# Handing out the mirror transposes of an attention kernel at two fixed keys of a block pair

## The chip, the cores and the metric

The kernel runs on one core of one Trainium2 chip. The metric is the device time of one execution in microseconds. A core has five engines that work side by side, each through its own queue in order: TensorE (PE, with its weight loads shown as PEld), VectorE (DVE), ScalarE (ACT), GpSimd (POOL) and SyncE (SP), which here only issues DMA transfers. Engines wait for each other and for transfers by semaphores.

## The reference

Eight batches of squared-relu attention without a softmax, gated by `u`, and then a mixture of experts over all 22528 tokens, with one dense expert and the best of eight gated ones:

```python
# u, v: (8, 2816, 256); z: (8, 2816, 64); scale = 1 / 2816
scores = scale * np.matmul(z, z.transpose(0, 2, 1))
attn = np.maximum(scores, 0.0) ** 2
x = (u * np.matmul(attn, v)).reshape(22528, 256)
y_dense = np.maximum(x @ w1_dense, 0.0) @ w2_dense
e = argmax(x @ w_gate);  gate = its softmax probability
out = y_dense + gate * (np.maximum(x @ w1[e], 0.0) @ w2[e])
```

The scores are those of `z` with itself, so `attn` is symmetric: the block of queries i and keys k is the transpose of the block of queries k and keys i.

## The kernel before, in words

**Tiles and groups.** A batch has 2816 positions, 22 blocks of 128 (`nK`). Queries are taken in groups of 2, 4, 4, 4, 4 and 4 blocks (`groups`), keys in blocks of 128. A group's squared scores stand in a buffer `A[n]` of 22 key blocks by up to 512 queries in bf16; three such buffers turn (`aA`, `bufs=3`), so group n+3 writes where group n was.

**Scores.** `scores` multiplies two key blocks with the queries of a group into a pair of PSUM banks (L383); `relu` offers two steps: the relu with the scale (ScalarE L398 or VectorE L400) into one of five `r` buffers, and the square (ScalarE L411, VectorE L413, or GpSimd in the first two groups) into `A[n]`. Four pairs of banks serve scores and outputs together.

**Mirror transposes.** Of a group n with n-2 in the same batch, the key blocks that belong to the queries of group n-2 aren't computed: they are the transposes of blocks that stand in `A[n-2]`. `far_steps(a)` makes the steps for that, four for each of the groups 0 to 3 of a batch; each is one DMA transpose, issued on SP (L446), that reads one key block of `A[a]` and writes columns of `A[a+2]`. There are 128 in the program. The last step of a group sets `key_at` for the mirrored blocks, the time at which the planner takes them as there.

**Outputs.** `av(n, i, ...)` multiplies a pair of query blocks (i, i+1) of group n with v: two halves (p = 0, 1) of 22 keys (x), four matmuls each (L552) with 64 rows. In the first half of a group's first pair the keys are taken in the order of their `key_at`. Between the keys it fills in scores of this group or the next two (`fill`). Behind a pair comes the gate (`gate_x`, VectorE L579), which multiplies the output by `u` into `pays` and then issues the transpose of the result on SP (L581, `xT`), which the router's logits (TensorE L607) need later.

**The order.** All engine queues but GpSimd's are in the order in which the Python code calls the instructions; a planner with a clock of its own (`now`, costs of the steps, `free`) decides while it runs which of the offered steps comes next and on which engine. At the start of `av`, `turning.extend(far_steps(n))` puts the group's four steps at the end of a list, and after a key the first of the list is taken, if the planner holds that its squares are done and that group a+1 is open.

**SP's queue.** It holds, in order, for every pair: the load of `u` for two pairs later (L146, three `ut` buffers, so it waits for the gate that frees one), the `xT` of an earlier pair (L581), the mirror transposes (L446), and twice a batch a transpose of z for the next batch (L116, `zT`), which waits for a copy on VectorE (L113).

**Then the mixture of experts.** Tokens are scattered by expert during the attention (GpSimd L697); after it, from about 562 us, the expert tiles are computed (L897 to L935). The change touches nothing there.

Of the kernel before, what the change touches and what calls it, by code (L numbers as in the profile page):

```python
# [19 lines left out]
def kernel(  # L20
# [63 lines left out]
    def banks(x, name, shape=(P, 2, 4 * P), dt=F32):  # L84

        return ps.tile(list(shape), dt, name=name, tag=f"b{x}")
# [46 lines left out]
    now = [0.0]  # L133
# [7 lines left out]
    def load_u(g, gate=False):  # L141
        ut = aw.tile([P, 2, D], F32, name="ut", bufs=3)
        if gate:
            nc.vector.memset(ut[:, 0, 0:1], 0.0)
        b, i = divmod(g, nK)
        nc.sync.dma_start(out=ut[:], in_=uf[:, b, i:i + 2, :])  # L146
        ut_of[g] = ut[:]
# [134 lines left out]
    def offer(ready, rank, ways, then=None):  # L282
        count[0] += 1
        todo.append((rank, count[0], ready, ways, then))
# [44 lines left out]
    def until(cond):  # L329

        while cond() is None:
            pick = best()
            assert pick is not None
            now[0] = max(now[0], pick[0][0])
            give(pick)
        now[0] = max(now[0], cond())
        run(now[0])

    def pe(t):
        now[0] += t  # L340
        run(now[0])


    left, far, key_at = {}, {}, {}
# [7 lines left out]
    def open_group(n):  # L352
        if n not in A:
            A[n] = aA.tile([P, nK, 4 * P], BF, name="A", tag="A")
# [6 lines left out]
    def take_pair():  # L361
        return pairs.pop(0)[1]

    def give_pair(t, x):
        pairs.append((t, x))
        pairs.sort()
# [64 lines left out]
    def can_turn(n, m):  # L431
        _, i0, w = groups[n]
        ts = [key_at.get((m, k)) for k in range(i0, i0 + w)]
        return None if None in ts else max(ts)

    def far_steps(a):

        n = a + 2
        if n >= len(groups) or far[n] != [a]:
            return []  # L440
        (b, i0, w), (_, j0, wj) = groups[n], groups[a]

        def step(i):
            assert n - 1 in A
            open_group(n)
            nc.sync.dma_start_transpose(out=A[n][:, j0:j0 + wj, i * P:(i + 1) * P],  # L446
                                        in_=A[a][:, i0 + i, :wj * P])
            if i == w - 1:
                for j in range(wj):
                    key_at[n, j0 + j] = now[0] + 10.0  # L450

        return [(a, lambda i=i: step(i)) for i in range(w)]

# [2 lines left out]
    def fill(n, force=False):  # L456

        if jobs and jobs[0][0] <= now[0] and room(1):
            jobs.pop(0)[1]()
            return True  # L460
        m = ahead(n)
        busy = sum(1 for op in todo if op[0] in (1, 4))
        if m is not None and room(1) and busy <= (4 if n < 2 else 2):
            scores(m, left[m].pop(0))
            return True
        return False
# [7 lines left out]
    def v_at(n, k):  # L474

        return 3.3 + 2.6 * (4 * k // nK) if n == 0 else 0.0

    def need(n, k):

        while max(key_at.get((n, k), 9e9), v_at(n, k)) > now[0]:  # L480
            if fill(n):
                continue
            pick = best()
            ts = [t for t, _ in pairs if t > now[0]]
            ts += [max(key_at[n, k], v_at(n, k))] if (n, k) in key_at else []
            assert pick is not None or ts
            if pick is not None and (not ts or pick[0][0] <= min(ts)):
                now[0] = max(now[0], pick[0][0])
                give(pick)
            else:  # L490
                now[0] = min(ts)
        run(now[0])

    turning = []
# [8 lines left out]
    def swap_rows(n):  # L503

        keep[0] = 0
        if ahead(n) is None:
            until(lambda: pairs[0][0] if pairs else None)
            x = take_pair()
            touch(x)
            touch(x)  # L510
            give_pair(now[0] + 0.1, x)
            return
        until(lambda: pairs[1][0] if len(pairs) > 1 else None)
        x = take_pair()
        touch(x)
        m = ahead(n)
        scores(m, left[m].pop(0))
        m = ahead(n)
        if m is None:
            touch(x)  # L520
            give_pair(now[0] + 0.1, x)
        else:
            scores(m, left[m].pop(0), x)

    def av(n, i, between):
        b, i0, w = groups[n]
        if i == i0:
            turning.extend(far_steps(n))
        keep[0] = 0
        if n == 0 and i == i0:  # L530

            fill(n)
            need(n, 0)
        until(lambda: pairs[0][0] if pairs else None)
        ox = take_pair()
        o = banks(ox, "o")
        for p in range(2):
            rest = list(range(nK))
            for x in range(nK):
                k = rest[0]  # L540
                if i == i0 and p == 0:

                    k = min(rest, key=lambda k: (max(key_at.get((n, k), 9e9), v_at(n, k)), k))
                    need(n, k)
                rest.remove(k)
                if n == 0 and i == i0 and p == 0 and x in (12, 14, 16):
                    load_u(2 * (x - 12) // 2, gate=True)
                for h in range(2):
                    r = slice(h * dq, (h + 1) * dq)
                    j = p ^ h  # L550
                    c = (i + j - i0) * P
                    nc.tensor.matmul(out=o[:, j, 0:D], lhsT=A[n][r, k, c:c + P],  # L552
                                     rhs=v_of[b][r, k, :], start=(p == 0 and x == 0),
                                     stop=(p == 1 and x == nK - 1))
                pe(0.1092)
                keep[0] = 2 - p if x >= nK - 12 else 0
                if x % 2 == 1 and x < nK - 1:
                    fill(n)
                if x % 7 == 3 and turning:
                    t = can_turn(turning[0][0] + 2, turning[0][0])  # L560
                    if t is not None and t <= now[0] and turning[0][0] + 1 in A:
                        turning.pop(0)[1]()
            if p == 0:
                swap_rows(n)
                between()

        def done(t):
            give_pair(t + 0.1, ox)

        g = b * nK + i  # L570
        offer(now[0] + 0.2, 0, {"dve": (0.63, lambda eng: gate_x(g, o))}, done)
        keep[0] = 0


    def gate_x(g, o):
        g0 = g % (2 * G)
        x = pays[:, g0:g0 + 2, 0:D]
        assert g + 1 < 2 * G or (g - 2 * G in placed and g + 1 - 2 * G in placed)
        nc.vector.tensor_mul(x, o[:, :, 0:D], ut_of.pop(g))  # L579
        xT = aw.tile([P, 5, P], BF, name="xT", bufs=8)  # L580
        nc.sync.dma_start_transpose(  # L581
            out=xT[:], in_=pays[:, g0:g0 + 2, :].rearrange("p n r -> p (n r)")[:, 0:5 * P])
        for j in range(2):
            xT_of[g + j] = xT[:, 3 * j:3 * j + 2, :]
# [512 lines left out]
    for n, (b, i0, w) in enumerate(groups):  # L1097
        for i in range(i0, i0 + w, 2):
            g = b * nK + i
            if 0 < g < nB - 4:  # L1100
                load_u(g + 4)
            av(n, i, lambda: tick(g))
            tick(g + 1)
# [7 lines left out]
    for s in range(NT - MAYBE + 2):  # L1111
# [4 lines left out]
        if s % 3 == 1 and waiting:  # L1116
# [5 lines left out]
    n = nc.values_load(used[0:1, 0:1], min_val=0, max_val=NH,  # L1122
                       skip_runtime_bounds_check_because="made by the table")
# [34 lines left out]
```

## Time and profile before

| | us |
|---|---|
| median of 3 runs | 886.56 |
| all three runs | 884.21, 886.56, 899.62 |
| the profiled execution | 887.47 |
| its span on the engines | 885.8 |

The profile is of one execution. A group row gives the line, the engine, the operation, what it writes and reads, the count, the busy time and the mean duration. A timeline row begins with start and duration in us; equal instructions that follow each other are merged into one row with their count, and square brackets hold the engine's idle time before the row and what ended it. A row of waits reads: who waited for whom, us in total, times, longest. SPq is SP's queue; its rows are issues, and a transfer lands later than its issue ends. The clock that TensorE was granted is 0.994 of full speed.

### The profile page before, as it was taken

How to read it: one execution, taken by the hardware profiler on the slowest of the kernel's cores; microseconds unless marked ns; L12 is line 12 of the kernel's file. 1: busy time of each engine (PE TensorE's matmuls, PEld its weight loads, DVE VectorE, ACT ScalarE, POOL GpSimd, SP SyncE). 2: the span in 40 equal slices, each digit the busy share in tenths (PEclk: the TensorE clock that was granted, in tenths of full speed). 3: DMA queues.
4: the chain of work that ended last, by engine and by line, in shares of the span. 5: the costliest groups of instructions: out<-in, count | busy, mean ns of one | idle time of the engine just before them, and what ended most of it. 6: DMA issues, size and time to landing. Idle time of an engine off the chain costs nothing.

```text
span 885.8 us, 30592 instructions
## 1 busy us (share of the span) xinstructions
PE 864.5 (98%) x12257; PEld 759.7 (86%) x12257; DVE 701.2 (79%) x1320; ACT 738.6 (83%) x913; POOL 485.2 (55%) x532
## 2 busy tenths in 40 slices
PE   8999999999998999999999999999999999999996
PEld 5788888898886888888888888888888888889996
DVE  7999999998996999999998997656665445546664
ACT  7999998998996998998998997477777777777774
POOL 8203343434533534434434544488888888887665
PEclk9999999999999999999999999999999999999998
DMA  6795997998898899899899896555565555544333
GB/s 148 148 174 117 146 185 145 172 174 170 153 165 168 154 181 190 127 197 198 131 196 172 151 159 112 103 133 128 129 132 122 117 120 121 123 113 110 97 100 82
DMA packets 257871, 127.64 MB, mean 144 GB/s; under 512 B 225470, under 2 KB 232894, under 8 KB 257728
## 3 DMA queue, kind: packets, MB, share of 16 engines
q1 hardware_dynamic: 230112, 70.24, 47.6%
q0 software_dynamic: 27616, 55.44, 29.2%
q8 instruction: 96, 1.57, 0.8%
q14 instruction: 47, 0.39, 0.2%
HBM read 61.54 MB, written 37.16 MB: 111 GB/s over the span
## 4 chain that ended last, share of the span: by engine, by line
PE 73%; DVE 7%; issue 6%; POOL 6%; DMA 4%; ACT 3%; SPq 0%; POOLq 0%; DVEq 0%; ACTq 0%
PE o L552 37%; PE h_ps L909 14%; PE yy L917 13%; PE s L383 8%; POOL out_dram L935 5%; DMA xT<-pays 3%; DVE r L400 2%; DVE A L413 2%; ACT A L411 1%; POOL A L413 1%; PE lg L607 1%; ACT r L398 1%; DVE pays L579 1%; DMA out_dram<-ring,ix 1%; DVE zn L113 1%
## 5 line engine op out<-in xcount | busy, mean ns | idle before, releaser
L552 PE MATMUL o<-vb,A 64*128 64x256 bf16 x7744 | 493.7, 270 | 2.6 <-POOL A L413 1.8
L552 PEld LDWEIGHTS <-A 64*128 64x128 bf16 x7744 | 408.1, 94 | 53.9 <-POOL A L413 3.0
L697 POOL DMA_INDIRECT xs<-pays,pi x176 | 196.9, 1119 | 271.1 <-DVE pi L695 207.1
L398 ACT ACTIVATE r<-s 128x1024 f32<-128x1024 f32 x274 | 270.0, 1011 | 26.1 <-PE s L383 22.1
L411 ACT ACTIVATE A<-r 128x1024 bf16<-128x1024 f32 (+1 forms) x257 | 261.3, 1042 | 5.3 <-DMA A<-A 2.7
L912 ACT ACTIVATE ring<-h_ps 128x1024 bf16<-128x1024 f32 x180 | 183.9, 1023 | 89.2 <-PE h_ps L909 87.3
L413 DVE TENSOR_TENSOR A<-r 128x1024 bf16<-128x1024 f32 x167 | 201.8, 1221 | 5.8 <-DMA A<-A 4.0
L400 DVE TENSOR_SCALAR r<-s 128x1024 f32<-128x1024 f32 (+1 forms) x158 | 190.5, 1214 | 4.3 <-POOL A L413 1.8
L933 DVE SCALAR_TENSOR_TENSOR ring<-yy,me,ring 128x256 f32<-128x256 f32 x180 | 86.8, 482 | 123.0 <-ACT ring L932 86.3
L935 POOL DMA_INDIRECT out_dram<-ring,me x140 | 146.4, 1046 | 39.8 <-issue 23.5
L383 PE MATMUL s<-zT 64*128 64x512 bf16 (+1 forms) x944 | 157.9, 359 | 1.6 <-ACT zT L192 0.6
L917 PEld LDWEIGHTS <-ring 128*128 128x128 bf16 x1440 | 140.0, 98 | 16.2 <-issue 0.3
L917 PE MATMUL yy<-w2d,ring 128*128 128x256 bf16 x720 | 108.0, 273 | 0.1
L917 PE MATMUL yy<-ring 128*128 128x256 bf16 x720 | 108.0, 273 | 0.0
L909 PE MATMUL h_ps<-ring,w1d 128*128 128x256 bf16 x720 | 93.3, 273 | 0.8 <-DVE pays L579 0.8
L909 PE MATMUL h_ps<-ring 128*128 128x256 bf16 (+1 forms) x880 | 93.7, 253 | 0.0
L897 DVE COPY ring<-wall 128x2048 bf16 x110 | 80.7, 748 | 8.6 <-DVE ring L933 4.2
L909 PEld LDWEIGHTS <-ring 128*128 128x128 bf16 x880 | 74.3, 98 | 6.8
L909 PEld LDWEIGHTS <-w1d 128*128 128x128 bf16 x720 | 70.1, 98 | 9.0 <-issue 1.0
L579 DVE TENSOR_TENSOR pays<-o,ut 128x512 bf16<-128x512 f32 x88 | 60.3, 685 | 17.6 <-PE o L552 17.1
L383 PEld LDWEIGHTS <-zT 64*128 64x128 bf16 x944 | 58.0, 94 | 16.0 <-issue 3.4
L932 ACT COPY ring<-yy 128x256 f32<-128x256 f32 x180 | 66.1, 367 | 1.8 <-PE yy L917 1.8
(120 smaller groups left out, 358.0 us busy)
## 6 DMA issues: line engine op xcount, KB each, us to landing
ut<-in_u_dram SPq DMA_DIRECT2D x88, 256.0 KB
vb<-in_v_dram POOLq DMA_DIRECT2D x16, 384.0 KB
vb<-in_v_dram POOLq DMA_DIRECT2D x16, 320.0 KB
wall<-in_moe_w_dram POOLq DMA_DIRECT2D x16, 256.0 KB
xs<-pays,pi POOLq DMA_INDIRECT x176
zr<-in_z_dram POOLq DMA_DIRECT2D x7, 352.0 KB
out_dram<-ring,me POOLq DMA_INDIRECT x140
A<-A SPq DMA_TRANSPOSE x128
```

The costliest lines, as they stand in the source:

```text
L383: nc.tensor.matmul(out=s[:, h, y * c:(y + 1) * c], lhsT=zT[r, k + h, :], rhs=zT[r, i0:i0 + w, :], start=True, stop=True)
L398: nc.scalar.activation(r[:, :, :c], s[:, :, :c], AF.Relu, scale=1.0 / S)
L400: nc.vector.tensor_scalar(out=r[:, :, :c], in0=s[:, :, :c], scalar1=1.0 / S, scalar2=0.0, op0=ALU.mult, op1=ALU.max)
L411: nc.scalar.activation(a, r, AF.Square)
L413: (nc.gpsimd if eng == "pool" else nc.vector).tensor_mul(a, r, r)
L552: nc.tensor.matmul(out=o[:, j, 0:D], lhsT=A[n][r, k, c:c + P], rhs=v_of[b][r, k, :], start=(p == 0 and x == 0), stop=(p == 1 and x == nK - 1))
L697: ins = nc.gpsimd.indirect_dma_start(out=xs, out_offset=bass.IndirectOffsetOnAxis(ap=pi[:], axis=0), in_=pays[:, g % (2 * G), 0:ROW].bitca ...
L909: nc.tensor.matmul(out=h_ps[:, f, hs, :], lhsT=w1(c, f), rhs=xT[:, hs, c, :], start=(c == 0), stop=(c == 1))
L912: nc.scalar.activation(h, h_ps[:].rearrange("p f h t -> p f (h t)"), AF.Relu)
L917: nc.tensor.matmul(out=y[:, k, :], lhsT=h[:, f, j * P:(j + 1) * P], rhs=w2(f), start=(f == 0), stop=(f == 3))
L933: nc.vector.scalar_tensor_tensor(out=ys, in0=y[:, 1, :], scalar=me[:, j, 0:1], in1=yd, op0=ALU.mult, op1=ALU.add)
L935: ins = nc.gpsimd.indirect_dma_start(out=out, out_offset=bass.IndirectOffsetOnAxis(ap=ids[j], axis=0), in_=ys, in_offset=None, bounds_chec ...
```

## The change

Two lines. A mirror transpose is handed out at key 3 of the first half and key 10 of the second half of a pair, so at most two a pair; before, it could be handed out at keys 3, 10 and 17 of either half, so at most six a pair and four in a row. And the mirrored key blocks count as there 6.0 us of the planner's clock after the last of a group's steps, before 10.0.

```diff
@@ far_steps
             if i == w - 1:
                 for j in range(wj):
-                    key_at[n, j0 + j] = now[0] + 10.0
+                    key_at[n, j0 + j] = now[0] + 6.0
@@ av
                 if x % 2 == 1 and x < nK - 1:
                     fill(n)
-                if x % 7 == 3 and turning:
+                if x == (3, 10)[p] and turning:
                     t = can_turn(turning[0][0] + 2, turning[0][0])
                     if t is not None and t <= now[0] and turning[0][0] + 1 in A:
                         turning.pop(0)[1]()
```

In the program that results, the instructions of TensorE, VectorE, ScalarE and GpSimd stand in the order of before; only SP's stand in another.

## The prediction

> **What bounds the kernel now.** I read the page first, for the engines' shares, then the stretches of 68 us in which one batch of attention runs, then the queue of SP and the rows of VectorE in one such stretch.
>
> ```profile
> span 885.8 us, 30592 instructions
> ...
> PE 864.5 (98%) x12257; PEld 759.7 (86%) x12257; DVE 701.2 (79%) x1320; ACT 738.6 (83%) x913; POOL 485.2 (55%) x532
> core 0: us, PE busy (x) PEld busy (x) DVE busy (x) ACT busy (x) POOL busy (x), PEclk, DMA share, GB/s
> 427.50:496.20 68.70, 67.33 (x1150) 59.03 (x1148) 64.16 (x115) 63.17 (x70) 31.17 (x31) 1.00 1.00 169
> ```
>
> TensorE is busy for 864.5 of the span's 885.8 us, so at most 21.3 us (2.4%) can be won by taking waits away. The seventh batch, 427.5 to 496.2 us, shows what stands beside TensorE: VectorE is idle for 68.70 - 64.16 = 4.5 us and ScalarE for 68.70 - 63.17 = 5.5 us. Three engines are nearly full there. Something that holds VectorE and ScalarE for longer than those 5 us in a batch comes out at the end.
>
> The change moves only DMA issues on SP. The order of instructions on the four other engines is the same before and after; so the question is what SP's later or earlier issues release, and when. Here is SP in that batch, with the gates (VectorE L579, one a pair of query blocks):
>
> ```profile
> 429.48 1.17 SPq L446 DMA_TRANSPOSE A<-A  x1
> 430.70 1.26 SPq L581 DMA_TRANSPOSE xT<-pays  x1
> 432.02 5.04 SPq L446 DMA_TRANSPOSE A<-A  x3
> 437.16 0.52 SPq L146 DMA_DIRECT2D ut<-in_u_dram  x1
> 437.73 1.21 SPq L581 DMA_TRANSPOSE xT<-pays  x1
> 439.42 5.64 SPq L446 DMA_TRANSPOSE A<-A  x4
> ...
> 450.15 5.12 SPq L446 DMA_TRANSPOSE A<-A  x4
> 455.36 2.21 SPq L116 DMA_TRANSPOSE zT<-zn  x1
> ...
> 465.07 5.13 SPq L446 DMA_TRANSPOSE A<-A  x4
> ...
> 473.88 1.74 SPq L581 DMA_TRANSPOSE xT<-pays  x1
> 433.88 0.69 DVE L579 TENSOR_TENSOR pays<-o,ut 128x512 bf16<-128x512 f32 x1 [0.20 <-PE o L552]
> 446.50 0.69 DVE L579 TENSOR_TENSOR pays<-o,ut 128x512 bf16<-128x512 f32 x1 [0.16 <-PE o L552]
> 458.93 0.68 DVE L579 TENSOR_TENSOR pays<-o,ut 128x512 bf16<-128x512 f32 x1
> 470.71 0.68 DVE L579 TENSOR_TENSOR pays<-o,ut 128x512 bf16<-128x512 f32 x1
> ```
>
> The reader is to see four sets of four mirror transposes (L446), one of each group 0 to 3, called T0 to T3 below: T0 is the 1 and the 3 from 429.48, T1 starts at 439.42, T2 at 450.15, T3 at 465.07. One issue takes about 1.26 us of SP (its row by line stands below), and each set goes out in one go. Every pair's load of u waits for the gate of the pair before, since three ut buffers turn; what stands behind such a load in SP's queue can't go out before that gate.
>
> **What the change removes, adds and moves.** It removes nothing and adds nothing: 128 mirror transposes remain. It hands out two in a pair, where up to four went out in one half. Four in a set need two pairs, and a set's first pair is the group's last (or only) one as long as the queue of sets runs behind, which it does from group 0 on: group 0 has one pair for its four. SP's order in one batch becomes, with a bar before each load of u:
>
> ```
> before: ut T0 xT T0 T0 T0 | ut xT T1 T1 T1 T1 | ut xT | ut xT T2 T2 T2 T2 zT | ut xT zT | ut xT T3 T3 T3 T3 | ut xT | ut xT
> after:  ut T0 xT T0 | ut xT T0 T0 | ut T1 xT T1 | ut xT T1 zT T1 | ut T2 xT zT T2 | ut xT T2 T2 | ut T3 xT T3 | ut T3 xT T3
> ```
>
> So the last T0 moves behind the load that waits for the gate at 433.88, one pair later than now; the last T1, T2 and T3 move two pairs later, behind the gates at 446.50, 458.93 and 470.71.
>
> Who waits for that: three A buffers turn. The transposes of group a read A[a], and the first squares of group a+3 (L411, L413) write into the same buffer, so they wait until all four have landed. A square that waits holds everything behind it on ScalarE or VectorE: the relus (L398, L400) that empty the score banks, and the gates. These are the first squares into the buffers of groups 0 to 3 now:
>
> ```profile
> 441.18 2.35 DVE L413 TENSOR_TENSOR A<-r 128x1024 bf16<-128x1024 f32 x2
> 455.06 1.06 ACT L411 ACTIVATE A<-r 128x1024 bf16<-128x1024 f32 x1
> 464.97 2.94 ACT L411 ACTIVATE A<-r 128x1024 bf16<-128x1024 f32 x3
> 474.97 1.22 DVE L413 TENSOR_TENSOR A<-r 128x1024 bf16<-128x1024 f32 x1
> ```
>
> None of the four waits; in the whole run only two of VectorE's squares do, 4.0 us in all. How long a transpose takes to land, the trace shows only where something waited for it:
>
> ```profile
> L446 SPq DMA_TRANSPOSE A<-A x128: 1160/1263/2849, 10.1 to 535.4; - x128
> DVE A L413 <- DMA A<-A: 4.0, 2, 3.2
> 122.92 3.90 SPq L446 DMA_TRANSPOSE A<-A  x3
> 132.63 1.23 DVE L413 TENSOR_TENSOR A<-r 128x1024 bf16<-128x1024 f32 x1 [0.77 <-DMA A<-A]
> 258.29 7.18 SPq L446 DMA_TRANSPOSE A<-A  x4
> 270.37 1.22 DVE L413 TENSOR_TENSOR A<-r 128x1024 bf16<-128x1024 f32 x1 [3.22 <-DMA A<-A]
> 478.52 0.20 PE L607 MATMUL lg<-wg,xT 128*128 128x8 bf16 x2 [1.28 <-DMA xT<-pays]
> ```
>
> From the end of the issue to the release that is 132.63 - 126.82 = 5.8 us, 270.37 - 265.47 = 4.9 us, and for an xT 478.52 - 475.62 = 2.9 us. The square at 441.18 did not wait for the T0 whose issue ended at 437.06, so there it was at most 4.1. The two long ones stand here because they were late; I take 3.5 us, nearer to the low end, and keep 2.9 and 4.9 for the range.
>
> The last transpose of a set then lands at: gate + 0.69 (its length) + 0.52 (load of u) + three transposes on SP (xT and two T, or T, xT and T) of 1.3 each with their gaps + 3.5, that is gate + 8.7 us (the first 0.1 is the release). For T1 a zT lies between, 2.0 more.
>
> - T0: 433.88 + 8.7 = 442.6, wanted at 441.2: 1.4 us late.
> - T1: 446.50 + 10.7 = 457.2, wanted at 455.1: 2.1 late.
> - T2: 458.93 + 8.7 = 467.6, wanted at 465.0: 2.6 late (ScalarE; VectorE's first is later).
> - T3: 470.71 + 8.7 = 479.4, wanted at 475.0: 4.4 late.
>
> All four buffers come free too late, 10.5 us in a batch. What of it TensorE loses: it works on while scores and banks last, but then both engines that empty the banks stand still, and those have only 4.5 and 5.5 us a batch to catch up. That idle time lies just behind T3's place, where the short two-block group has little to square: VectorE has 1.54 us there, ScalarE 1.92 and 2.29:
>
> ```profile
> 478.76 0.25 DVE L617 TENSOR_REDUCE m<-lg 128x11 f32<-128x88 f32 x1 [1.54 <-PE lg L607]
> 479.33 0.28 ACT L621 ACTIVATE ex<-d 128x88 f32<-128x88 f32 x1 [1.92 <-DVE d L619]
> 484.79 1.94 ACT L398 ACTIVATE r<-s 128x1024 f32<-128x1024 f32 x2 [2.29 <-PE s L383]
> ```
>
> So I let T3's 4.4 vanish in ScalarE's 4.2 and count the other three in full: 1.4 + 2.1 + 2.6 = 6.1 us a batch, 8 batches, 49 us. Each stall shifts the gates with it, so it comes again in the next batch rather than wearing off.
>
> Against it stands a gain. The four in a row also hold up the xT transposes behind them, and TensorE's logits wait for those:
>
> ```profile
> PE lg L607 <- DMA xT<-pays: 6.6, 4, 4.2
> ```
>
> With fewer transposes ahead of an xT some of the 6.6 us goes; bounds are 0 and 6.6, I take 3, as xT still has one T ahead of it in some pairs. The smaller key (10.0 to 6.0 after the hand-out) sorts keys only in the planner, and leaves the order of the matmuls as it was: nothing, and no cover is needed. Sum: 49 - 3 = 46 us. The profiled execution took 887.47 us, 0.9 above the median of 886.56; 887.5 + 46 = 933 us.
>
> **Rivals.** *The transposes land early enough, and only the gain is left* (not slower). If a transpose landed 1.0 us behind its issue, the four would be there at 440.1, 454.7, 465.1 and 476.9: T3's 1.9 us falls into the idle time, the others cost 0.1 or nothing, and the 6.6 us of waits for xT go: 881 us, to 888 if they stay. It decides from a landing of about 1.5 us downward. Against it: the shortest seen above is 2.9. The Trainium skill, "DMA: Bandwidth & Descriptors", section on the anatomy of one DMA, fits the time of a DMA as about 2.0 us plus its bytes at 436 GB/s; by that fit (made for another issuing path) a 128 KB transpose would land 2.3 us behind the start of its issue, an estimate from that page, and this rival would hold. The trace disagrees, with 4.6 us from the start of the xT at 473.88 to its release. I give this rival 0.13.
>
> *The mirrored rows themselves come late, and TensorE waits at L552.* Group a+2 multiplies with what T of group a wrote. T0's 442.6 is wanted by the pair that starts at the gate of 446.50, T1's 457.2 at 458.93, T2's 467.6 at 470.71. The least room is 1.7 us, and the mirrored keys come late in the planner's sort. It decides where landings go above 5.2 us, with T1 first; at 5.8 it would be 0.6 us in each batch, 5 us on top of stalls that would then be 6.1 + 3 x 2.3 = 13 us a batch, 104 us: 990 us. I give it 0.06.
>
> *T3 isn't hidden either*: the idle time is ScalarE's wait for TensorE and moves along with it. Then 10.5 us in each of seven batches (the last has no successor for T3) and 6.1 in the last: 80 us, 965 us. This is the upper part of my own case; 0.2 of its chance lies there.
>
> **How the numbers follow.** Forecast, stalls at the squares: 0.81, of this 0.2 near 965. Early landing 0.13, late rows 0.06. Within the forecast the landing sets the size: at 2.9 it is (6.1 - 1.8) x 8 = 34, less the whole 6.6: 915 us; at 4.9 it is (6.1 + 4.2) x 8 = 82: 970 us. The range 904 to 970 takes these in and leaves out most of the first rival and all of the second, some 0.19. Two per cent of the time before is 17.7 us, about what a measurement of this kernel can tell from no change. Faster by that would need 17.7 of TensorE's 21.3 idle us: 0.02. Within it: the early landing with the smallest stalls, 0.13. Slower: 0.85.
>
> **What would show it.** In the profile after, squares L411 and L413 should have idle time ended by the DMA A<-A, some 3 to 5 times a batch, 2 to 4 us each, at group changes; that row now says 4.0 us in all for VectorE. The stretch of a batch should grow from 67 to 73 us, with TensorE's busy time unchanged in it. The stretch behind the attention should take as long as now. Waits for xT should shrink. If the squares show no such idle time, the landing was sized wrong; if they show it and the batch is still 67 us long, the room on ScalarE and VectorE was.

## The result and the profile after

The changed kernel takes 971.84 us (median of 4 runs, 965.51 to 979.47), the kernel before beside it 885.38 us (4 runs): a ratio of 1.10, 95% interval 1.0912 to 1.1087. Ratios, here and below, are of runs in the chip's faster state alone, so they are not always the quotient of the medians given. The profiled execution took 972.19 us. The forecast was 933 us in a range of 904 to 970: the direction is right, the size is not.

The page of the changed kernel, its shares and its groups of squares:

```profile
span 970.5 us, 30581 instructions
PE 890.7 (92%) x12257; PEld 771.6 (80%) x12257; DVE 700.6 (72%) x1320; ACT 738.7 (76%) x913; POOL 481.5 (50%) x532
L411 ACT ACTIVATE A<-r 128x1024 bf16<-128x1024 f32 (+1 forms) x257 | 261.5, 1043 | 77.2 <-DMA A<-A 75.5
L413 DVE TENSOR_TENSOR A<-r 128x1024 bf16<-128x1024 f32 x167 | 202.1, 1222 | 83.4 <-DMA A<-A 68.6
```

VectorE and ScalarE do the same work in the same busy time as before (700.6 and 738.7 us, before 701.2 and 738.6). What is new stands behind the second bar: idle time ahead of the squares, ended by the mirror transposes. TensorE's busy time has grown by 26 us with the same 12257 matmuls. That was not forecast.

The stretches before and behind the end of the attention (the last L552), and single batches, first of the kernel before (the eighth batch), then of the changed one (the seventh and the eighth; span of the stretch, busy time and count by engine, granted clock, DMA share):

```profile
0.00:562.10 562.10, 548.85 (x9197) 475.34 (x9198) 517.51 (x924) 506.63 (x551) 235.15 (x244) 0.99 0.94 161
562.10:885.80 323.70, 315.63 (x3062) 284.41 (x3060) 183.72 (x396) 231.93 (x362) 250.10 (x289) 0.99 0.50 116
496.20:562.00 65.80, 64.96 (x1116) 55.70 (x1112) 55.24 (x132) 50.15 (x56) 28.62 (x27) 1.00 0.80 134
```

```profile
0.00:646.80 646.80, 575.03 (x9197) 487.21 (x9198) 518.92 (x924) 506.79 (x551) 232.51 (x244) 0.96 0.82 139
646.80:970.50 323.70, 315.65 (x3062) 284.43 (x3060) 181.73 (x396) 231.93 (x362) 248.96 (x289) 0.99 0.52 116
498.00:580.10 82.10, 71.36 (x1150) 60.76 (x1148) 64.22 (x115) 63.51 (x70) 30.40 (x31) 0.96 0.88 142
580.10:646.60 66.50, 65.07 (x1118) 55.72 (x1112) 55.47 (x132) 49.84 (x56) 28.64 (x27) 1.00 0.75 131
```

All of the 84.7 us lies in the attention; the part behind it takes 323.7 us in both. Within the attention TensorE's idle time grows from 562.10 - 548.85 = 13.3 to 646.80 - 575.03 = 71.8 us (58.5 more), and its busy time by 26.2 us, while its granted clock falls from 0.99 to 0.96. The seventh batch takes 82.10 us where it took 68.70; the eighth and last, 66.50 where it took 65.80, is hardly longer.

The seventh batch closer, in timeline rows of the changed kernel: the first squares into the buffers of groups 0 to 3 on VectorE, then on ScalarE, then the rows of TensorE that waited.

```profile
517.15 2.36 DVE L413 TENSOR_TENSOR A<-r 128x1024 bf16<-128x1024 f32 x2 [5.37 <-DMA A<-A]
534.17 1.23 DVE L413 TENSOR_TENSOR A<-r 128x1024 bf16<-128x1024 f32 x1 [2.44 <-DMA A<-A]
548.54 1.22 DVE L413 TENSOR_TENSOR A<-r 128x1024 bf16<-128x1024 f32 x1 [2.50 <-DMA A<-A]
561.17 1.22 DVE L413 TENSOR_TENSOR A<-r 128x1024 bf16<-128x1024 f32 x1 [2.25 <-DMA A<-A]
517.11 1.06 ACT L411 ACTIVATE A<-r 128x1024 bf16<-128x1024 f32 x1 [2.38 <-DMA A<-A]
534.13 1.06 ACT L411 ACTIVATE A<-r 128x1024 bf16<-128x1024 f32 x1 [2.58 <-DMA A<-A]
548.50 2.95 ACT L411 ACTIVATE A<-r 128x1024 bf16<-128x1024 f32 x3 [4.53 <-DMA A<-A]
561.15 1.06 ACT L411 ACTIVATE A<-r 128x1024 bf16<-128x1024 f32 x1 [1.85 <-DMA A<-A]
520.76 0.40 PE L552 MATMUL o<-vb,A 64*128 64x256 bf16 x4 [3.78 <-DVE r L400]
536.64 0.39 PE L383 MATMUL s<-zT 64*128 64x512 bf16 x2 [2.08 <-DVE r L400]
552.41 0.61 PE L552 MATMUL o<-vb,A 64*128 64x256 bf16 x4 [3.51 <-ACT r L398]
563.05 0.39 PE L383 MATMUL s<-zT 64*128 64x256 bf16 x4 [1.24 <-DVE pi L695]
```

Four times in the batch both engines that empty the score banks stand still until the same event, and 2 to 3 us after the second of them has stopped TensorE stops too. In three of the four rows its releaser is a relu (L400, L398), which empties a bank, and in the fourth another VectorE instruction (L695); in none is it the DMA. Nothing of TensorE's own row names the cause; one has to follow it back through its releaser to the square ahead of that. The row of waits of the kernel before, `PE lg L607 <- DMA xT<-pays: 6.6, 4, 4.2`, has no successor: the waits for xT are gone.

SP's queue in that batch, with the last issue of T0 (506.94), T1 (529.49), T2 (541.57) and T3 (557.27), and the load of the next batch's z on GpSimd:

```profile
506.94 2.51 SPq L446 DMA_TRANSPOSE A<-A  x2
511.75 0.33 SPq L146 DMA_DIRECT2D ut<-in_u_dram  x1
517.07 1.66 SPq L446 DMA_TRANSPOSE A<-A  x1
...
529.49 1.50 SPq L446 DMA_TRANSPOSE A<-A  x1
...
541.57 4.28 SPq L446 DMA_TRANSPOSE A<-A  x2
...
557.27 1.27 SPq L446 DMA_TRANSPOSE A<-A  x1
507.17 0.59 POOL L106 DMA_DIRECT2D zr<-in_z_dram  x1
```

The last T0 has been issued at 506.94 + 2.51 = 509.45 us, and the squares start at 517.11: 7.7 us of landing. The last T1 has been issued at 530.99, its squares start at 534.13: 3.1 us. The load of z goes out at 507.17, ahead of the last T0 (the second of the two from 506.94), and that T0 lands behind it.

### The profile page after: what moved, and what is told of

Its sections match the earlier page's. It is cut to its first block, busy times and chain, and to the rows that moved or that the text cites. A ratio compares the mean times of both kernels' runs of the same rounds, so it can differ in the third digit from the quotient of the medians.

```text
span 970.5 us, 30581 instructions
## 1 busy us (share of the span) xinstructions
PE 890.7 (92%) x12257; PEld 771.6 (80%) x12257; DVE 700.6 (72%) x1320; ACT 738.7 (76%) x913; POOL 481.5 (50%) x532
## 4 chain that ended last, share of the span: by engine, by line
PE 47%; DMA 15%; issue 12%; ACT 9%; DVE 7%; POOL 6%; SPq 2%; POOLq 0%; DVEq 0%; ACTq 0%
PE o L552 19%; DMA A<-A 13%; PE h_ps L909 12%; PE yy L917 11%; POOL out_dram L935 5%; PE s L383 5%; ACT r L398 4%; ACT A L411 4%; DVE r L400 2%; DVE A L413 2%; SPq L446 1%; DVE pays L579 1%; SPq L581 1%; DMA out_dram<-ring,ix 1%; POOL A L413 1%
## 5 line engine op out<-in xcount | busy, mean ns | idle before, releaser
L552 PE MATMUL o<-vb,A 64*128 64x256 bf16 x7744 | 512.2, 276 | 34.1 <-ACT r L398 17.1
L552 PEld LDWEIGHTS <-A 64*128 64x128 bf16 x7744 | 418.4, 96 | 94.2 <-issue 39.9
L697 POOL DMA_INDIRECT xs<-pays,pi x176 | 194.5, 1105 | 349.4 <-DVE pi L695 268.4
L398 ACT ACTIVATE r<-s 128x1024 f32<-128x1024 f32 x274 | 269.6, 1011 | 26.7 <-PE s L383 25.1
L400 DVE TENSOR_SCALAR r<-s 128x1024 f32<-128x1024 f32 (+1 forms) x158 | 190.9, 1216 | 16.5 <-PE s L383 14.0
L383 PE MATMUL s<-zT 64*128 64x512 bf16 (+1 forms) x944 | 163.0, 371 | 31.3 <-ACT r L398 12.5
L383 PEld LDWEIGHTS <-zT 64*128 64x128 bf16 x944 | 60.0, 96 | 51.9 <-issue 37.6
L897 DVE COPY ring<-wall 128x2048 bf16 x110 | 78.7, 730 | 9.0 <-DVE ring L933 4.4
```

The source lines that it names most:

```text
L383: nc.tensor.matmul(out=s[:, h, y * c:(y + 1) * c], lhsT=zT[r, k + h, :], rhs=zT[r, i0:i0 + w, :], start=True, stop=True)
L398: nc.scalar.activation(r[:, :, :c], s[:, :, :c], AF.Relu, scale=1.0 / S)
L400: nc.vector.tensor_scalar(out=r[:, :, :c], in0=s[:, :, :c], scalar1=1.0 / S, scalar2=0.0, op0=ALU.mult, op1=ALU.max)
L697: ins = nc.gpsimd.indirect_dma_start(out=xs, out_offset=bass.IndirectOffsetOnAxis(ap=pi[:], axis=0), in_=pays[:, g % (2 * G), 0:ROW].bitca ...
```

## The experiments

Seven kernels ran on another chip, where the kernel before takes 927.96 us (e1 to e4) and 927.5 us (e5 to e7) instead of 885 us, because what follows the attention takes some 364 us there in place of 324; e8 and e9 ran where it takes 885.49 us. The attention takes about as long on both (562.1 us in e2 there, 562.1 before here). So what is compared below is the ratio to the kernel before on the same chip and the end of the attention; absolute times that were expected by the first chip's 886 us are some 40 us low for that reason.

**e1: the changed order, but the transposes read another tile.** The mirror transposes go out in the changed order, but read a tile of noughts and not A[a], so no square has to wait for them. Left out: the mirrored blocks are noughts, and the two dense weight matrices share a tile, to make room.

```diff
+    nought = const.tile([P, 4 * P], BF, name="nought")
...
-                                        in_=A[a][:, i0 + i, :wj * P])
+                                        in_=nought[:, :wj * P])
```

> The changed kernel, but the mirror transposes read a tile of noughts in place of A[a] (the mirrored scores are nought, and the two dense weight matrices share one tile; both are left out of the true computation). Number, size, destinations and hand-out of the transposes stay as in the changed kernel. Theory S (the squares of group a+3 wait for the landing of the late transposes that read the buffer they write to): nothing reads A[a] any more, so the squares' idle time of 76 us (ScalarE) and 69 us (VectorE) goes to under 5 us each, TensorE's granted clock rises from 0.973 to 0.99, and the time falls to 878 to 892 us. Rival M (the mirrored rows land late, and TensorE waits for them at L552) and rival Q (SP's queue in the new order holds up loads and xT): destination and order are unchanged, so the time stays above 950 us.

Measured: ratio 0.9993, interval 0.9957 to 1.0029; the attention ends at 560.9 us (562.1 before, 646.8 after the change). No row of waits names the mirror transposes, which are A<-nought there. Its attention:

```profile
0.00:560.90 560.90, 549.47 (x9197) 474.31 (x9198) 517.31 (x924) 506.51 (x551) 233.58 (x244) 1.00 0.95 161
```

All of the loss hangs on the read of A[a]: the same issues in the same places cost nothing once no square waits for them. TensorE's busy time is back at 549 us and its clock at 1.00, so the 26 us of busy time are a consequence of the same waits, not a cost of their own.

**e2: the same on the kernel before**, with the same parts left out, as a control for e1.

> The kernel before with the same edit as the run before it (transposes of noughts, left out as there). It is the control. Theory S: the two engines' idle time for A<-A, 6.7 us in all, goes, and the time is 878 to 888 us. If the reading of A cost more than the waits show, it would fall below 870 us.

Measured: 1.0023, 0.9992 to 1.0054; the attention ends at 562.1 us. Taking the read away is worth nothing where nothing waits for it, so e1 shows the wait and not a cheaper transfer.

**e3: group 0 hands out four in its one pair, all else as changed.** The prediction said that each set is late because group 0 has one pair for its four and every later set runs behind it.

```diff
-                if x == (3, 10)[p] and turning:
+                if (x == (3, 10)[p] or i0 == 0 and x in (3, 10)) and turning:
```

> The changed kernel, but group 0 of a batch, which has one pair alone, hands out at keys 3 and 10 of both halves, so four in its pair; all other groups at one per half as in the change. Then no set is left over for the next group, and each set ends one pair earlier. Theory S: the last transposes of T0 to T3 stand behind the gates one pair earlier and land about 6 us earlier, in front of the squares; stalls of at most 1 to 2 us a batch stay; 882 to 900 us. Rival P (the pace of one per half is what costs): seven of eight pairs keep the pace, so more than half of the loss stays: above 930 us.

Measured: 1.010, 1.0066 to 1.0134; the attention ends at 579.2 us, so 67.6 of the 84.7 us are back in the profiled execution; by the medians, 939.80 beside 927.96, some 12 us are left. The rows of waits of e3:

```profile
DVE A L413 <- DMA A<-A: 15.5, 6, 3.6
ACT A L411 <- DMA A<-A: 15.1, 9, 3.4
```

Nearly all that is left of them lies at one place, T3 against the first squares of the next batch's group 0, with up to 3.6 us, where 1 to 2 were expected. One pair of backlog, made in group 0 and handed on from set to set, is most of the change's cost; at most two a pair by itself is not.

**e4: the same two a pair, both in the first half.** It keeps the number per pair and takes away the later key.

```diff
-                if x == (3, 10)[p] and turning:
+                if p == 0 and x in (3, 10) and turning:
```

> The changed kernel with both of a pair's hand-outs in the first half (keys 3 and 10 of p = 0, none in p = 1). Theory S: a set still closes in the first pair of the next group, behind the same gate, and the order on SP within a pair hardly changes; 955 to 980 us. Rival K (the late key in the second half is what makes them late): the hand-out comes about 6 us earlier, and the loss falls to under a third: below 915 us.

Measured: 1.088, 1.0796 to 1.0964; the attention ends at 642.9 us. That is no gain that can be told: two executions of the changed kernel itself end their attention at 646.8 and 642.1 us (e9). A hand-out half a pair earlier that leaves the last of a set behind the same load of u, as this one does on SP, leaves the loss as it is, and one that puts it in front of that load (e3) takes most of it away. So what counts is the load of u, and with it the gate, behind which the last of the set stands.

**e5: the loads of z for the batches 2 to 7 left out.** These batches compute their scores with the z of batch 1, so the output differs, and the part behind the attention has one more expert tile; the attention's instructions are the same but for the loads. It tests what made the landing of T0 so long.

```diff
-        nc.gpsimd.dma_start(out=z_of[b][:], in_=z[b].rearrange("(p k) d -> p k d", p=P))
+        if b == 1: nc.gpsimd.dma_start(out=z_of[b][:], in_=z[b].rearrange("(p k) d -> p k d", p=P))
```

> The changed kernel without the loads of z for batches 2 to 7 (their scores are made of batch 1's z; this is left out). In the changed kernel the last two T0 land 8.7 us behind their issue, while the 352 KB load of z for the next batch is on the way. Theory Z (the two share the DMA engines, so T0 is late by some 4 us more than its place in the queue makes it): VectorE's longest stall of a batch, 5.4 us at the first square of group 3, falls to about 2 us in these batches, and the attention ends at 610 to 630 us in place of 646.6. Rival (the landing is long because of SP's own load of u and xT in front): the stall stays near 5 us and the attention ends at 640 to 648 us.

Measured: 1.0794, 1.072 to 1.0867; the attention ends at 628.3 us, 18.5 us sooner than with the change alone (13.8 sooner than in e9, the changed kernel once more). T0 and the first square of group 3 in the seventh batch of e5, then its stretch of attention:

```profile
492.49 2.48 SPq L446 DMA_TRANSPOSE A<-A  x2
498.42 2.36 DVE L413 TENSOR_TENSOR A<-r 128x1024 bf16<-128x1024 f32 x2 [0.95 <-DMA A<-A]
0.00:628.30 628.30, 569.38 (x9197) 485.04 (x9198) 518.87 (x924) 507.04 (x551) 227.84 (x238) 0.97 0.79 140
```

Without the load the last T0 is there 498.42 - 494.97 = 3.5 us behind its issue, and not 7.7 (the expectation's 8.7 are counted from about the start of that issue, these from its end); the square's wait falls from 5.37 to 0.95 us. The other three sets wait as before (2.4 to 2.7 us each on VectorE). Of the 18.5 us, 646.80 - 628.30, TensorE's busy time gives 575.03 - 569.38 = 5.7.

**e6: groups 0 and 3 hand out four a pair, groups 1 and 2 two.** e3 left T3 late; here it goes out a pair sooner too.

```diff
-                if x == (3, 10)[p] and turning:
+                if (x == (3, 10)[p] or n % 6 in (0, 3) and x in (3, 10)) and turning:
```

> The changed kernel, but groups 0 and 3 of a batch hand out at keys 3 and 10 of both halves; groups 1 and 2 at one per half. Against the run in which only group 0 did so, T3 goes out one pair earlier, as before the change. Theory S: the stall at the first square of the next batch's group 0, 2 to 3.6 us in each batch of that run, goes; the attention ends at 558 to 566 us (578.9 in that run, 561.8 before), and the time is 0.995 to 1.005 of the kernel before. If spreading T1 and T2 has a worth of its own (fewer waits of TensorE for xT), it is 0.99 to 0.995. Rival P (the pace as such costs): above 1.01.

Measured: 1.0057, 1.0026 to 1.0088; the attention ends at 563.5 us, against 562.1 before. The waits for A are down to 1.5 us on ScalarE and 0.5 on VectorE, and those for xT to 2.4. Nearly all of the loss in the attention is undone, and no gain is left: the ratio is clear of 1 and a little over the 1.005 that was expected. What the last half per cent is, no run here shows.

**e7: the other way, on the kernel before.** Any odd key may hand out a transpose, so a set goes out sooner than before.

```diff
-                if x % 7 == 3 and turning:
+                if x % 2 == 1 and turning:
```

> The kernel before, but a mirror transpose is handed out after any odd key in place of keys 3, 10 and 17: the other way than the change, as early and as close in a row as the planner lets them. Theory S: the squares that still wait before (6.7 us of idle time in all, batches 2 and 3) wait less; TensorE's waits for xT stay, as more transposes go out in front of an xT; attention ends at 556 to 563 us, ratio 0.99 to 1.0. Rival B (transposes in a row hold up loads and xT, which the change meant to mend): slower than before, 1.005 to 1.02.

Measured: 1.0035, 1.0004 to 1.0067; the attention ends at 561.6 us. It is slower by a third of a per cent, between what theory and rival gave. There is nothing to win in this direction: the kernel before has hardly any of these waits left to take away.

**e8: the number alone**, on the kernel before.

```diff
-                    key_at[n, j0 + j] = now[0] + 10.0
+                    key_at[n, j0 + j] = now[0] + 6.0
```

> The kernel before with the key alone changed (mirrored blocks count as there 6.0 instead of 10.0 us after the hand-out); the hand-out stays at keys 3, 10 and 17. Theory: the number costs nothing that shows. Within a group's first half some mirrored keys are multiplied a few matmuls earlier, the transposes go out as before, so no square waits: attention ends at 560 to 564 us, ratio to the kernel before 0.997 to 1.004, waits of VectorE and ScalarE for A under 5 us each. Rival: the earlier matmuls at L552 run into transposes that have not landed; then TensorE's waits at L552 for the DMA A<-A show up, some 1 to 3 us a batch, attention 570 to 585 us, ratio 1.01 to 1.025, and that part of the change's loss belongs to the number.

Measured: 1.0011, 0.9961 to 1.0061; medians 883.03 and 885.49 us. The attention of the profiled execution ends at 556.2 us, 4 us under the expected span, and the waits for A are 0.5 us. No wait of TensorE for the DMA A<-A appears. The number costs nothing that can be measured. The later hand-out without the number was not run; but in e1 the number stays in the changed order, and nothing of the loss is left.

**e9: the changed kernel once more**, to have it beside the other runs. It ran where the kernel before takes 885 us, as in the first runs, so its comparison of two chips was not made.

> The changed kernel itself on the chip of the experiments, so that the runs that alter it have it beside them. Theory: the loss lies in the attention alone, which takes the same time on both chips: attention ends at 640 to 650 us, VectorE's and ScalarE's waits for A at 60 to 80 us each, and the time is that chip's kernel before plus 80 to 90 us. Rival: what comes behind the attention adds to the loss or hides some of it on this chip; then the difference of the times lies 10 us or more away from the difference of the ends of attention.

Measured: 1.0985, 1.0877 to 1.1093; 970.6 us. The attention ends at 642.1 us, the rest takes 323.6 us, the waits for A are 69.9 and 63.6 us: the loss and its place repeat.

No version here is faster than the kernel before.

## Why the prediction was right in kind and wrong in size

**The mechanism held.** The first squares into a buffer wait until the transposes that read it have landed (e1), the sets are late by the pair that group 0 can't use (e3), the gate behind which the last transpose stands is what counts (e3 and e4), the number costs nothing (e8), and the part behind the attention is unchanged.

One premise was wrong, without harm to the sum: that TensorE's instructions keep their order. The order of the keys goes by `key_at`, and the hand-out moves that too. In all 32 first halves that use mirrored blocks the keys stand in another order, and in 31 of them the mirrored ones that `key_at` was set for now come last of the 22; before, they stood further forward. The other three engines do keep their order. The number by itself pulls those keys forward, which e8 shows to be harmless. The later hand-out pushes them back by more, and so late rows had more room than the prediction counted.

**First step that failed: T0's landing, "I take 3.5 us, nearer to the low end".** One landing was used for all four sets. In the seventh batch it took, from the end of the issue to the squares, 3.1 us for T1, 548.50 - 545.85 = 2.65 for T2 and 561.15 - 558.54 = 2.6 for T3 (rows of SP above); these three fit the range of 2.9 to 4.9 or are a little better. (In the batches two to seven as a whole they spread from 2.3 to 5.0.) T0 took 7.7, and so its squares were 5.4 us late in place of 1.4. The prediction moved T0 a pair later without asking which transfers run there. The load of z, 352 KB, stood in the kernel before here:

```profile
436.65 0.59 POOL L106 DMA_DIRECT2D zr<-in_z_dram  x1
```

The last T0 had been issued by 437.06 us then, so all but its end was out ahead of the load; now the load goes out at 507.17, ahead of the last T0. e5 takes the load away, and the landing is 3.5 us. The changed kernel has such a case of its own: the last batch loads no z for a next one, and its last T0 is there 594.71 - 591.43 = 3.3 us behind its issue, where the six batches before it, all with the load, show 5.0 to 7.7.

```profile
588.95 2.48 SPq L446 DMA_TRANSPOSE A<-A  x2
594.71 2.00 ACT L411 ACTIVATE A<-r 128x1024 bf16<-128x1024 f32 x2 [0.78 <-DMA A<-A]
```

The sign was there before. The prediction put its two long landings, 5.8 and 4.9 us, down to having been late. In both, a load of v (384 or 320 KB) had been issued while those transposes, from 122.92 and from 258.29 us, were going out:

```profile
125.29 0.57 POOL L129 DMA_DIRECT2D vb<-in_v_dram  x1 [0.21 <-issue]
262.07 0.58 POOL L129 DMA_DIRECT2D vb<-in_v_dram  x1 [0.21 <-issue]
```

No run here leaves out a load of v, so that these were the cause is not shown.

By the forecast's own count, 1.4 + 2.1 + 2.6 = 6.1 us a batch, with T3 hidden. TensorE's four waits in the seventh batch are 3.78, 2.08, 3.51 and 1.24, in sum 10.6 us: T1 as forecast, T0 2.4 more, T2 0.9 more, and T3 not wholly hidden: its squares were 2.25 us late in place of 4.4, and half of that shows on TensorE. T2 was late although it landed fast: the last two issues took SP 4.28 us (row of 541.57), where the forecast had 1.3 each.

The seventh batch is one of those that lose most. Over the whole attention the idle time grew by 58.5 us, 7.3 a batch, and in the eighth, which the forecast counted with 6.1 like the others, by 0.6 (66.50 - 65.07 and 65.80 - 64.96). The sum had 46 (49 less 3 for xT; all 6.6 of that went), so 12.5 us of the miss are idle time. By e5 the loads of z account for 11 to 13 us of idle time: 71.8, or 69.8 in e9, against 628.30 - 569.38 = 58.9. That this nearly equals the 12.5 is in part luck, since the eighth batch lost less than was counted and T3, counted with nothing, cost something.

**Second step that failed: "with TensorE's busy time unchanged in it".** This is worth 26 us, twice the first. After a long wait TensorE's matmuls run at half speed for a while. Two waits of the changed kernel, in windows with the granted clock in the third figure from the right (the window of 3.41 us is one whole stretch of half clock):

```profile
271.35 0.40 PE L552 MATMUL o<-vb,A 64*128 64x256 bf16 x4 [2.57 <-DVE r L400]
271.30:272.00 0.70, 0.61 (x6) 0.23 (x7) 0.63 (x3) 0.24 (x2) 0.10 (x1) 1.00 0.44 88
272.00:275.40 3.40, 3.40 (x38) 2.41 (x36) 3.31 (x8) 3.40 (x5) 1.51 (x2) 0.58 0.39 89
521.74:525.15 3.41, 3.41 (x34) 2.25 (x32) 3.39 (x7) 3.41 (x4) 1.76 (x2) 0.50 0.51 119
522.00:525.40 3.40, 3.40 (x36) 2.29 (x34) 3.24 (x7) 3.38 (x5) 1.76 (x2) 0.54 0.51 127
525.40:528.00 2.60, 2.60 (x45) 2.00 (x41) 1.98 (x3) 2.60 (x3) 0.99 (x1) 1.00 1.22 148
65.84 0.61 PE L383 MATMUL s<-zT 64*128 64x512 bf16 x4 [3.28 <-ACT r L398]
65.80:69.20 3.40, 3.36 (x58) 3.15 (x59) 1.81 (x3) 3.40 (x4) 0.53 (x1) 1.00 1.02 117
```

After the wait of 2.57 us that ends at 271.35 the clock stays full for 0.7 us and is then 0.58 over 3.40 us, in which 38 matmuls run; after the wait of 3.78 us shown above it is 0.54 in a like stretch and full again from 525.4 us. After the 3.28 us that end at 65.84 nothing happens. Of the 14 waits of TensorE of 2.5 us or more behind the first 60 us, twelve go with a stretch of half clock of 3.41 us, two of these with a double one: 14 x 3.41 x 0.5 = 24 us of work lost at most, since a few of the stretches begin within the wait. The kernel before has one such stretch, at its wait of 4.19 us for xT that ends at 273.52, so 22 of the 24 are new. By the mean clock it is 970.5 x (1 - 0.973) - 885.8 x (1 - 0.994) = 21 us. So each such stretch cost up to 1.7 us on top of the wait. That the loss follows the waits is shown by e1, where busy time and clock are as before; that the halved clock is all of the 26 us is not, since 21 to 22 are accounted for.

The prediction did not price this. The Trainium skill, "TensorE: Matmul & The Clock Gate", Part 1, says that TensorE falls to 1.2 GHz after at least one idle window of about 3.4 us. The trace agrees on the half speed (0.50), and its stretches are 3.41 us long. It does not agree on the idle time that it takes: a wait of 2.57 us was enough once. No sharp length shows in these runs, for in e3 a wait of 1.42 us that ends at 494.21 was enough (clock 0.50 from 494.80 to 498.10), and here 3.28 us was not.

**The rivals.** The early landing falls: in the changed kernel, behind the first batch, no square that waited was released less than 2.3 us behind the last issue of its set (284.48 - 282.17), and in the first batch only one was, at 75.23 - 73.68 = 1.55 us. The Trainium skill's fit in "DMA: Bandwidth & Descriptors", in the anatomy of one DMA (2.3 us from the start of the issue, an estimate from that page, whose fit is for another issuing path), is short of the trace's 1.50 + 3.1 = 4.6 us for the last T1. Late mirrored rows fall: no wait at L552 names the DMA A<-A, though the sets were later than forecast; the new order of the keys gave them room. The rival that T3 isn't hidden gave 965 us, near the result, but for a wrong reason: T3 cost TensorE 1.2 to 2.9 us in five batches and 0.7 or less in the other three, and the rest came from T0 and the clock. The 972 us lie just above the range of 904 to 970, whose upper end was made from landing times alone.

## What to carry to other kernels

Before a transfer is moved, list what other queues send at its new place: its landing time there is not the one that it had at the old place (7.7 us beside a 352 KB load, 3.5 without). Limiting how often a queue may be fed is harmless only as long as the shortest group still gets its share out; one group that falls a step behind hands the backlog to all that follow. And where waits of some us on TensorE come in, price each at its own length plus up to 1.7 us of halved clock: of 14 waits of 2.5 us or more here 12 had it, and now and then a shorter one does.

## What was unexpected of the hardware

The same program takes 885 us on one chip and 928 us on another, with nearly all of the difference behind the attention. No trace of the kernel before itself is from the second chip, but e6 ends its attention there at 563.5 us, beside 562.1, and takes 364.3 us behind it, where its instructions are those of before, against 323.7; TensorE was busy for 324.1 and 315.6 us of these. Nothing here was tried to find out why. A single 352 KB load more than doubled the landing of a transpose issued beside it.
